# Two-way attention and a two-layer network on one core: the reads' rows reordered and moved ahead of the last token tiles, under a new list of steps

## The chip, the cores and the metric

The kernel runs on one core of a Trainium2 chip. The metric is the device time of one execution in microseconds, lower is better. A core has TensorE (PE in the profile; PEld is its weight load), VectorE (DVE), ScalarE (ACT), GpSimd (POOL), and SyncE (SP), which here only issues DMAs. The DMAs of SP, ACT and POOL run on 16 shared DMA engines. SBUF is the working memory, PSUM holds what PE writes, in eight banks of 2 KB for each of 128 partitions.

## The reference

For each of 8 batches and 8 heads, 512 tokens `x` and 32 states (64 columns each) read one another; the reads of all heads, side by side, pass through two matrices with a PReLU between them.

```python
scores = scale * np.matmul(x, state.transpose(0, 1, 3, 2))
a = softmax(scores); xread = np.matmul(a, state)      # each token reads the states
scores2 = scale * np.matmul(state, x.transpose(0, 1, 3, 2))
a2 = softmax(scores2); sread = np.matmul(a2, x)       # each state reads the tokens
y = np.concatenate([xread, sread], axis=2)            # 8 batches of 512 + 32 rows of 512
h = y @ w_in                                          # 512 -> 2048
g = np.maximum(h, 0.0) + alpha * np.minimum(h, 0.0)
return g @ w_out                                      # 2048 -> 512, 4352 rows
```

## The kernel before

All work is written out by hand as a list, `ORDER`: each token of it (`F.3.1.4`) calls a step with its arguments, and each engine executes its instructions in the order in which the list brings them. Waits between engines follow from the tiles. When an engine waits, all that stands behind it on that engine waits too. Two reads of one PSUM tile by different engines also follow one another in the list's order.

PSUM is given out by number: a step's last figures are banks 0 to 5 (`single`), and one tile of two banks (`two`) serves the scores and some of the `m` steps in turn. A step that takes a bank waits for the last reader of what stood in it.

The steps, for a batch b (0 to 7):
- `lx` loads x (POOL's queue, cast to f16), `wi` and `wo` the four parts of each weight matrix. `xt`/`xo` transpose x on PE and copy it out (batches 0 and 1), `xd` transposes it by a DMA of SP's queue (batches 2 to 7). `stt`, `sto`, `str`, `sro` do the same with the states.
- `sc` computes the scores, states as weights (small matmuls on parts of the array). For the tokens' softmax over the states: `sb` (DVE, blocks transposed), `smax`, `ssh` (subtraction), `sexp` (ACT), `ssum` (sum and reciprocal), `snorm` (POOL or DVE, as the letter says), `wb` (transposed back). Batch 0 does these in two halves of 256 tokens (last figure 0 or 1).
- For the states' softmax over the tokens: `tm` (maximum, DVE), `te` (exponential, ACT), `tsum`, `tn` (POOL), `tt` (a DMA transpose on SP's queue, into the tile `e2T`), `rd` (32 small matmuls, `sr_ps`), `rdo` (copied into `XS`).
- The tokens' reads are never formed: `m` multiplies the states with a quarter f of `w_in` (16 quarter tiles, `mo` copies them out: `mo.b.f.e` in one piece on engine a = ACT or v = DVE, `mo.b.f.e.g` in halves), and the first layer is then attention weights times `m`.
- `F.b.jc.k` (first) makes 128 of the 2048 hidden columns for 512 tokens: two matmuls of 512 columns into bank k. `N` (ACT) takes max(-h, 0), `G` (DVE) adds it, scaled, to h and so frees the bank. `b = 8` stands for the 256 rows of state reads, from `XS`: four matmuls of 256 columns.
- `S.b.q.i` (second) adds hidden columns 2i and 2i+1 to output tile q of 128 tokens: two matmuls of 512 columns. `O` copies the tile out and stores it on SP's queue (256 KB). `R.q.i` and `RO.q` do so for the two tiles of state reads.

Before, the last steps are the token tiles of batch 7, then `R` and `RO`. `RO` copies half of a tile on ACT and half on DVE into one tile `osr` and stores it, 4 batches by 32 states.

Of the kernel before, what the change touches and what calls it, by code (L numbers as in the profile page):

```python
# [17 lines left out]
stc lst stt.0 oma wi.0 sto.a wo.0 xt.0.0.1.0 wi.1 xt.0.0.0.1 xo.0.0.1.v lx.1 xo.0.0.0.v xt.0.1.0.0  # L18
sc.0.0 wo.1 xo.0.1.0.v xt.0.1.1.1 sb.0.0 wi.2 xo.0.1.1.a smax.0.0 wi.3 sc.0.1 str.1.1 sb.0.1
ssh.p.0.0 tm.0 str.0.0 sro.1.a wo.2 smax.0.1 sexp.0.0 m.0.0.1.2 lx.2 sro.0.a ssh.v.0.1 ssum.0.0  # L20
sexp.0.1 m.1.0.0.3 mo.0.0.a.0 mo.0.0.a.1 m.2.0.4.5 snorm.p.0.0 ssum.0.1 te.0.1 m.3.0.1.2 snorm.p.0.1
wb.0.0 te.0.0 lx.3 wb.0.1 mo.1.0.a.0 mo.1.0.a.1 m.4.0 tsum.0 mo.2.0.a.0 mo.2.0.a.1 tn.0.1 F.0.0.0
mo.3.0.a.0 mo.3.0.a.1 m.0.1.4.5 wo.3 F.0.1.3 N.0.0 mo.0.1.a.0 mo.0.1.a.1 tn.0.0 G.0.0 F.0.2.1 N.0.1
F.0.3.0 xt.1.0.0.4 N.0.2 G.0.1 xt.1.1.1.5 tt.0 xt.1.0.1.2 xo.1.0.0.a G.0.2 xo.1.1.1.a F.0.4.3
S.0.0.0.4 N.0.3 xo.1.0.1.v F.0.5.1 N.0.4 G.0.3 xt.1.1.0.2 mo.4.0.a S.0.2.0.5 xo.1.1.0.v S.0.0.1
G.0.4 N.0.5 F.0.6.2 sc.1 G.0.5 N.0.6 m.1.1.3.0 S.0.2.1 mo.1.1.a.0 mo.1.1.a.1 sb.1 F.0.7.1 S.0.2.2
N.0.7 m.0.2.0.3 G.0.6 S.0.0.2 mo.0.2.a.0 mo.0.2.a.1 smax.1 S.0.1.0.2 S.0.1.1 F.0.8.0 G.0.7 ssh.p.1
S.0.1.2 N.0.8 tm.1 S.0.3.0.3 F.0.9.1 S.0.1.3 N.0.9 G.0.8 S.0.3.1 sexp.1 S.0.2.3 G.0.9 F.0.10.0
# [6 lines left out]
N.1.5 S.1.0.1 N.1.6 S.0.1.6 G.1.4 te.2.1 S.0.1.7 G.1.5 F.1.7.5 O.0.1.a m.2.2 G.1.6 N.1.7 F.1.8.1
tsum.2 mo.2.2.a rdo.1.v S.1.1.0.2 tn.2.0 G.1.7 F.1.9.3 N.1.8 smax.2 S.1.1.1 N.1.9 F.1.10.5 xd.4
tn.2.1 S.1.0.2 N.1.10 G.1.8 m.2.1 S.1.0.3 G.1.9 mo.2.1.a F.1.11.1 ssh.p.2 G.1.10 S.1.1.2 N.1.11
F.1.12.3 F.1.13.5 G.1.11 tt.2 N.1.12 S.1.1.3 N.1.13 F.1.14.1 G.1.12 sexp.2 m.2.3 G.1.13 S.1.0.4
F.1.15.3 mo.2.3.a ssum.2 S.1.0.5 S.1.1.4 N.1.14 S.1.1.5 N.1.15 G.1.14 sc.3 snorm.p.2 rd.2.5 xd.5
G.1.15 S.1.0.6 sb.3 S.1.0.7 S.1.1.6 lx.6 O.1.0.a S.1.1.7 wb.2 m.3.1.3.1 S.1.2.0.4 S.1.2.1 rdo.2.v  # L40
smax.3 F.2.0.5 F.2.1.0 N.2.0 S.1.2.2 tm.3 ssh.p.3 N.2.1 S.1.2.3 S.1.2.4 S.1.2.5 G.2.0 te.3.1 S.1.2.6
O.1.1.v S.1.2.7 sexp.3 F.2.2.5 G.2.1 S.1.3.0.2 O.1.2.a ssum.3 S.1.3.1 N.2.2 S.1.3.2 te.3.0 F.2.4.4
S.1.3.3 G.2.2 snorm.p.3 N.2.4 F.2.3.0 tsum.3 mo.3.1.v.0 mo.3.1.v.1 S.1.3.4 N.2.3 F.2.5.5 S.1.3.5
N.2.5 tn.3.1 G.2.4 S.1.3.6 S.1.3.7 G.2.5 F.2.8.4 O.1.3.a G.2.3 m.3.2 tn.3.0 N.2.8 m.3.3.5.1 F.2.6.2
wb.3 mo.3.3.a.0 mo.3.3.a.1 F.2.9.0 S.2.0.0.3 N.2.6 tt.3 G.2.8 S.2.0.1 N.2.9 S.2.1.0.1 G.2.6 F.2.7.4
G.2.9 S.2.1.1 N.2.7 F.2.10.2 mo.3.2.v F.2.11.0 N.2.10 S.2.0.2 N.2.11 S.2.1.2 G.2.7 rd.3.5 G.2.10
F.2.12.4 rdo.3.a lx.7 G.2.11 S.2.0.3 N.2.12 F.2.13.5 S.2.1.3 G.2.12 N.2.13 S.2.0.4 F.2.14.4 G.2.13
S.2.0.5 N.2.14 S.2.1.4 F.2.15.5 G.2.14 S.2.1.5 N.2.15 S.2.0.6 sc.4 G.2.15 S.2.1.6 xd.6 sb.4 S.2.0.7
F.3.0.5 O.2.0.a S.2.1.7 tm.4 N.3.0 F.3.1.4 S.2.2.0.3 N.3.1 F.3.4.0 G.3.0 te.4.1 S.2.2.1 smax.4
S.2.2.2 N.3.4 F.3.2.5 te.4.0 S.2.2.3 G.3.1 ssh.p.4 N.3.2 S.2.2.4 S.2.2.5 G.3.4 F.3.5.4 G.3.2 F.3.3.0  # L50
N.3.5 S.2.2.6 O.2.1.v N.3.3 F.3.6.5 G.3.5 sexp.4 S.2.3.0.1 S.2.3.1 G.3.3 N.3.6 S.2.3.2 tsum.4 ssum.4
# [528 lines left out]
```

## Time and profile before

| | |
|---|---|
| median of 3 runs | 230.43 us (229.63 to 230.91) |
| profiled execution | 230.58 us, its span 228.8 us |
| PE busy | 210.5 us (92%) |
| DVE, ACT, POOL busy | 164.9 (72%), 140.5 (61%), 72.0 (31%) |
| first `F` matmul, last matmul's end | 17.39 us, 220.97 us |

The span runs from the first to the last instruction; 1.8 us of the execution's time lie around it. The idle time of an engine counts only where it delays the end; the chain of waits follows the end back to what released it.

### The profile page before, as it was taken

The page shows a single profiled execution, that of the slowest core. Times are in us where ns is not written, and L with a number is a line of the kernel's source. Part 1 is how long each engine was busy: PE and PEld are TensorE (multiplying, and loading weights), DVE is VectorE, ACT ScalarE, POOL GpSimd, SP SyncE. Part 2 cuts the span into 40 slices and gives each one's busy share as a digit, 9 for nine tenths or more (in the row PEclk, how much of TensorE's full clock was granted, in tenths as well). Part 3 has the DMA queues.
Part 4 walks back from the last instruction along what each step waited for, and adds up shares of the span by engine and source line. Part 5 has one row for each costly group of instructions (what it writes and reads, how often), then busy time and mean ns, then how long its engine had stood idle before and what let it go on. Part 6 is the DMA issues. An engine that isn't in the chain of part 4 may idle for free.

```text
span 228.8 us, 4077 instructions
## 1 busy us (share of the span) xinstructions
PE 210.5 (92%) x1584; PEld 96.5 (42%) x1584; DVE 164.9 (72%) x245; ACT 140.5 (61%) x261; POOL 72.0 (31%) x57
## 2 busy tenths in 40 slices
...
GB/s 69 184 200 199 201 181 192 190 225 185 167 167 106 95 80 149 50 134 56 89 46 138 3 92 0 114 28 47 49 92 47 3 92 0 61 34 92 92 34 57
DMA packets 49051, 23.11 MB, mean 101 GB/s; under 512 B 40456, under 2 KB 44680, under 8 KB 49032
## 3 DMA queue, kind: packets, MB, share of 16 engines
...
q14 instruction: 7, 0.06, 0.1%
...
## 4 chain that ended last, share of the span: by engine, by line
PE 82%; DVE 8%; DMA 3%; ACT 2%; issue 1%; POOL 1%; SPq 0%; POOLq 0%; ACTq 0%
PE o L498 44%; PE h L458 24%; PE m_ps L421 4%; PE h L467 3%; PE o L518 3%; DMA xg<-in_x_dram 2%; PE sr_ps L396 2%; DVE nb L352 2%; DVE gt L486 1%; DMA e2T<-e 1%; PE xT_ps L259 1%; DVE ts L304 1%; PE sc L274 1%; DVE r L328 1%; DVE nb L355 1%
## 5 line engine op out<-in xcount | busy, mean ns | idle before, releaser
L498 PE MATMUL o<-w_out_sb,gt 128*128 128x512 f16 x512 | 130.5, 379 | 0.0
L486 DVE SCALAR_TENSOR_TENSOR gt<-neg,oma_sb,h 128x512 f16<-128x512 f32 x128 | 90.7, 736 | 22.9 <-ACT neg L478 21.6
L478 ACT ACTIVATE neg<-h 128x512 f32<-128x512 f32 (+1 forms) x144 | 80.0, 579 | 40.7 <-PE h L458 34.4
L458 PE MATMUL h<-aT,m 128*128 128x512 f16 x256 | 75.1, 387 | 1.0 <-DVE gt L486 0.7
L498 PEld LDWEIGHTS <-gt 128*128 128x128 f16 x512 | 48.7, 98 | 57.6 <-issue 3.6
L458 PEld LDWEIGHTS <-m 128*128 128x128 f16 x256 | 24.4, 99 | 32.5 <-issue 6.0
L318 POOL TENSOR_TENSOR ts<-ts,mx 128x1024 f32<-128x1024 f32 (+1 forms) x8 | 14.4, 1800 | 53.5 <-DVE mx L312 53.5
L377 POOL TENSOR_SCALAR e<-e,r 128x512 f16<-128x512 f16 x16 | 24.9, 1562 | 5.3 <-DVE r L373 3.0
L508 ACT COPY osb<-o 128x512 f32<-128x512 f32 x25 | 14.5, 591 | 18.7 <-PE o L498 18.4
L332 POOL TENSOR_TENSOR an<-ts,r 128x1024 f16<-128x1024 f32 (+1 forms) x9 | 15.4, 1718 | 22.1 <-DVE r L329 15.5
L421 PE MATMUL m_ps<-w_in_sb,stT 64*32 64x512 f16 x256 | 13.4, 425 | 2.0 <-ACT stT L241 1.3
L447 ACT CAST m<-m_ps 128x512 f16<-128x512 f32 x26 | 13.9, 609 | 1.7 <-PE m_ps L421 1.7
L445 ACT CAST m<-m_ps 128x1024 f16<-128x1024 f32 x13 | 13.2, 1014 | 0.8 <-PE m_ps L421 0.6
L508 DVE COPY osb<-o 128x512 f32<-128x512 f32 x7 | 4.8, 685 | 11.6 <-PE o L498 11.6
L157 POOL DMA_DIRECT2D xg<-in_x_dram x7 | 8.4, 1199 | 12.8 <-PE sr_ps L396 12.8
L363 ACT ACTIVATE e<-sc,nb 128x512 f16<-128x512 f32 x16 | 11.0, 689 | 2.2 <-DVE gt L486 1.2
L304 DVE STREAM_TRANSPOSE ts<-sc 128x1024 f32<-128x1024 f32 x7 | 8.7, 1246 | 3.7 <-PE sc L274 2.9
L340 DVE STREAM_TRANSPOSE aT<-an 128x1024 f16<-128x1024 f16 (+1 forms) x9 | 10.1, 1119 | 1.4 <-POOL an L332 1.2
L328 DVE TENSOR_REDUCE r<-ts 128x32 f32<-128x1024 f32 (+1 forms) x9 | 9.8, 1090 | 1.0 <-ACT ts L324 1.0
L352 DVE TENSOR_REDUCE nb<-sc 128x2 f32<-128x1024 f32 x8 | 9.7, 1208 | 0.5 <-PE sc L274 0.5
L312 DVE TENSOR_REDUCE mx<-ts 128x32 f32<-128x1024 f32 (+1 forms) x9 | 9.8, 1089 | 0.0
L467 PE MATMUL h<-XS,w_in_sb 128*128 128x256 f16 x64 | 8.9, 273 | 0.0
...
## 6 DMA issues: line engine op xcount, KB each, us to landing
out_dram<-osb SPq DMA_DIRECT2D x32, 256.0 KB, 2.0
...
xg<-in_x_dram POOLq DMA_DIRECT2D x2, 256.0 KB, 5.0
out_dram<-osr SPq DMA_DIRECT2D x2, 256.0 KB
...
e2T<-e SPq DMA_TRANSPOSE x8, 3.1
```

Of the source, the lines that this page charges most:

```text
L318: engine(e).tensor_tensor(ts, ts, over_blocks(cols(live["mx", b], j, S // N)), ALU.subtract)
L332: engine(e).tensor_tensor(blocks(cols(live["an", b], j, S)), blocks(cols(live["ts", b], j, S)), over_blocks(cols(live["r1", b], j, S // N) ...
L352: nc.vector.tensor_reduce(nb, live["sc", b].rearrange("p r j g s -> p g (r j) s"), AX.XY, ALU.max)
L377: nc.gpsimd.tensor_scalar_mul(e2, e2, live["r2", b][:, g : g + 1])
L421: nc.tensor.matmul(t[N * k : N * (k + 1), :], st_head(b, h)[64 * r : 64 * r + 64, :], w_in_sb[64 * r : 64 * r + 64, c, 512 * f : 512 * (f ...
L447: copier(e)(m_tile(b)[:, f, g, :], t[g])
L458: nc.tensor.matmul(h.rearrange("p (r j s) -> p r j s", r=2, j=2), ms[b][:, f, g, 128 * j : 128 * (j + 1)], weights(b, g), start=(g == 0), ...
L467: nc.tensor.matmul(h, w_in_sb[:, c, 128 * jc : 128 * (jc + 1)], XS[:, c, :, :].rearrange("p b n -> p (b n)"), start=(c == 0), stop=(c == n ...
L478: nc.scalar.activation(neg, h, RELU, bias=0.0, scale=-1.0)
L486: nc.vector.scalar_tensor_tensor(gt, negs.pop((b, jc)), oma_sb[:, jc : jc + 1], h, ALU.mult, ALU.add)
L498: nc.tensor.matmul(outs[b, q], gts[b, jc][:, 128 * q : 128 * (q + 1)], w_out_sb[:, jc, :], start=(jc == 0), stop=(jc == n_jc - 1),)
L508: copier(e)(osb, outs.pop((b, q)))
```

## The change

- All places in `ORDER` are new: the steps are nearly the same, but their order, PSUM banks and engines (a, v, p) are others.
- Three `F` steps of batch 0 become six `f` steps (`first_part`), each for one half of 256 tokens, so that the first half needs only `wb.0.0`.
- `XS` keeps the state reads as (half of the batches, state, batch in the half), so output tile q of `R` has its 128 rows in the order state, batch. `RO` copies a whole tile on one engine, and its store goes by 32 states, 4 batches.
- `R` and `RO` stand between the `S` steps of batch 7. The last step is now `O.7.3.s`: two halves of the columns, one copied by ACT and stored from ACT's queue, one copied by DVE and stored from SP's.

```diff
-    XS = consts.tile([128, n_c, B, N], F16)
+    XS = consts.tile([128, n_c, 2, N, B // 2], F16)
...
-        copier(e)(XS[:, :, b, :], live.pop(("sr", b)))
+        copier(e)(XS[:, :, b // 4, :, b % 4], live.pop(("sr", b)))
...
-                    XS[:, c, :, :].rearrange("p b n -> p (b n)"),
+                    XS[:, c].rearrange("p q n b -> p (q n b)"),
...
+    def first_part(b, jc, j, k=None):
+        if ("part", b, jc) not in live:
+            live["part", b, jc] = hs[b, jc] = single(k, f"h_{b}_{jc}", [128, S], F32)
+        f, i = divmod(jc, 4)
+        for g in range(2):
+            nc.tensor.matmul(
+                hs[b, jc].rearrange("p (r j s) -> p r j s", r=2, j=2)[:, :, j, :],
+                ms[b][:, f, g, 128 * i : 128 * (i + 1)],
+                weights(b, g)[:, :, j, :],
...
     def second_out(b, q, e):
...
+        if e == "s":
+            for i, (c, n) in enumerate((("a", nc.scalar), ("v", nc.sync))):
+                osb = moe.tile([128, w], F32, name=f"osb_{b}_{q}_{i}", tag="osr", bufs=2)
+                copier(c)(osb, t[:, w * i : w * (i + 1)])
+                n.dma_start(rows[:, w * i : w * (i + 1)], osb)
+            return
...
-    def second_reads_out(q):
-        w = d_model // 2
-        osb = moe.tile([128, d_model], F32, name=f"osr_{q}", tag="osr", bufs=2)
-        nc.scalar.copy(osb[:, :w], outs[B, q][:, :w])
-        nc.vector.tensor_copy(osb[:, w:], outs[B, q][:, w:])
-        nc.sync.dma_start(out.rearrange("(b s) d -> b s d", s=S2)[4 * q : 4 * (q + 1), S:], osb)
+    def second_reads_out(q, e):
+        osb = moe.tile([128, d_model], F32, name=f"osr_{q}", tag="osb", bufs=4)
+        copier(e)(osb, outs.pop((B, q)))
+        rows = out.rearrange("(b s) d -> b s d", s=S2)[4 * q : 4 * (q + 1), S:]
+        nc.sync.dma_start(rows.rearrange("b n d -> n b d"), osb)
```

Of the list, the end reads now:

```diff
-S.7.3.7 R.0.0.0 O.7.3.v R.0.1 R.0.2 R.0.3 R.0.4 R.0.5 R.0.6 R.0.7 R.1.0.2 RO.0 R.1.1 R.1.2 R.1.3
-R.1.4 R.1.5 R.1.6 R.1.7 RO.1
+S.7.2.3 R.1.6 S.7.2.4 R.1.7 S.7.2.5 RO.1.v S.7.2.6 S.7.2.7 S.7.3.0.2 O.7.2.v S.7.3.1 S.7.3.2 S.7.3.3
+S.7.3.4 S.7.3.5 S.7.3.6 S.7.3.7 O.7.3.s
```

**The end, DVE's queue.** `osr` are the read tiles, `osb` the token tiles, `o_7_3` the PSUM tile of the last token step; the brackets name whom a row waits for. Before:

```order
L486 SCALAR_TENSOR_TENSOR gt_7_14_2809<-neg_7_14_2799,oma_sb_84,h_7_14_2790 128x512 [waits Activation_49]
L486 SCALAR_TENSOR_TENSOR gt_7_15_2817<-neg_7_15_2811,oma_sb_84,h_7_15_2803 128x512 [waits Activation_49]
L508 COPY osb_7_3_2887<-o_7_3_2852 128x512 [waits DMAHW3_49,DMAHW7_49,DMAHW1_49,PE_49]
L530 COPY osr_0_2907<-o_8_0_2884 128x256 [waits Activation_49]
L530 COPY osr_1_2925<-o_8_1_2904 128x256 [waits Activation_49]
```

After:

```order
L501 SCALAR_TENSOR_TENSOR gt_7_11_2835<-neg_7_11_2828,oma_sb_84,h_7_11_2823 128x512 [waits Activation_49]
L550 COPY osr_0_2853<-o_8_0_2805 128x512 [waits DMAHW3_49,DMAHW6_49,DMAHW0_49,PE_49]
L550 COPY osr_1_2913<-o_8_1_2874 128x512 [waits DMAHW5_49,DMAHW3_49,DMAHW7_49,DMAHW2_49,PE_49]
L532 COPY osb_7_2_2923<-o_7_2_2896 128x512 [waits DMAHW4_49,DVE_49,PE_49]
L528 COPY osb_7_3_1_2943<-o_7_3_2920 128x256 [waits Activation_49]
```

The last half copy on DVE waits for ACT in both; the tile is now a token tile, and the read tiles stand ahead of it.

**The start, DVE's queue, batch 0.** `r1` are the sums of the two halves, `an` the normalized weights, `aT` the weights turned back (`wb`). Before:

```order
L328 TENSOR_REDUCE r1_0_146<-ts_0_144 128x16 [waits Activation_49]
L329 RECIPROCAL r1_0_146<-r1_0_146 128x16 [waits DVE_49]
L328 TENSOR_REDUCE r1_0_146<-ts_0_144 128x16 [waits Activation_49]
L329 RECIPROCAL r1_0_146<-r1_0_146 128x16 [waits DVE_49]
L340 STREAM_TRANSPOSE aT_0_148<-an_0_147 128x512 [waits Pool_49] x2
L373 RECIPROCAL r2_0_253<-r2_0_253 128x2 [waits Activation_49]
```

After:

```order
L329 TENSOR_REDUCE r1_0_146<-ts_0_144 128x16 [waits Activation_49]
L330 RECIPROCAL r1_0_146<-r1_0_146 128x16 [waits DVE_49]
L341 STREAM_TRANSPOSE aT_0_148<-an_0_147 128x512 [waits Pool_49]
L333 TENSOR_TENSOR an_0_147<-ts_0_144,r1_0_146 128x512 [waits DVE_49]
L374 RECIPROCAL r2_0_261<-r2_0_261 128x2 [waits Activation_49]
L341 STREAM_TRANSPOSE aT_0_148<-an_0_147 128x512 [waits DVE_49]
L446 CAST m_4_293<-m_ps4_0_271 128x1024 [waits PE_49]
```

The second half's normalization moved from POOL to DVE, between the two transposes, and a cast of `m` follows.

**The start, ACT's queue.** `ts` are the exponentials of the two halves (`sexp`), `m_0` the casts `mo.0.0`. Before:

```order
L324 ACTIVATE ts_0_144<-ts_0_144 128x512
L447 CAST m_0_236<-m_ps0_0_0_209 128x512
L447 CAST m_0_236<-m_ps0_0_1_210 128x512
L363 ACTIVATE e2_0_252,r2_0_253<-sc_0_120,nb_0_187 128x512 x2
L447 CAST m_1_271<-m_ps1_0_0_226 128x512
```

After:

```order
L448 CAST m_0_223<-m_ps0_0_0_210 128x512
L448 CAST m_0_223<-m_ps0_0_1_211 128x512
L325 ACTIVATE ts_0_144<-ts_0_144 128x512
L364 ACTIVATE e2_0_260,r2_0_261<-sc_0_120,nb_0_203 128x512 x2
L448 CAST m_1_268<-m_ps1_0_0_228 128x512
```

The second half's exponential now stands behind the two casts.

**Batch 2's transposes, SP's queue.** Before:

```order
L511 DMA out_0_dram<-osb_0_1_779 128x512
L251 DMA_TRANSPOSE xT_4_820<-xg_4_732 128x16x128
L381 DMA_TRANSPOSE e2T_2_861<-e2_2_742 128x8x128
L251 DMA_TRANSPOSE xT_5_957<-xg_5_745 128x16x128
L511 DMA out_0_dram<-osb_1_0_975 128x512
```

After:

```order
L533 DMA out_0_dram<-osb_0_3_775 128x512
L382 DMA_TRANSPOSE e2T_2_869<-e2_2_704 128x8x128
L252 DMA_TRANSPOSE xT_4_884<-xg_4_778 128x16x128
L252 DMA_TRANSPOSE xT_5_981<-xg_5_798 128x16x128
L533 DMA out_0_dram<-osb_1_0_998 128x512
```

`e2T_2`, which the state reads of batch 2 need, changed places with `xT_4`.

## Rows read from the trace of the kernel before

**Rows 1.** The page's busy time of each engine (us, share of the span, instructions)

```profile
PE 210.5 (92%) x1584; PEld 96.5 (42%) x1584; DVE 164.9 (72%) x245; ACT 140.5 (61%) x261; POOL 72.0 (31%) x57
```

**Rows 2.** The chain in order of time: start us, us, what

```profile
17.39 1.03 PE h L458 x2
...
19.08 2.67 PE h L458 x6
...
22.70 0.43 PE h L458 x2
...
151.37 0.54 PE o L498 x2
...
214.04 6.92 PE o L518 x32
...
220.99 0.38 ACT osr L529
...
221.39 0.42 DVE osr L530
```

**Rows 3.** Windows: stretch, its us, busy us of each engine, PEclk, DMA

```profile
19.08:21.75 2.67, 2.67 (x8) 0.99 (x9) 1.12 (x2) 2.67 (x6) 2.63 (x3) 1.00 1.27 206
...
62.20:130.00 67.80, 67.76 (x493) 29.97 (x494) 60.06 (x85) 44.66 (x83) 23.13 (x14) 1.00 0.48 97
142.00:201.00 59.00, 59.00 (x429) 29.24 (x428) 45.94 (x74) 39.76 (x76) 10.65 (x7) 1.00 0.17 55
```

**Rows 4.** Timeline of PE: start us, us, instruction, [idle before and releaser]

```profile
50.58 0.59 PE L458 MATMUL h<-aT,m 128*128 128x512 f16 x2 [0.65 <-DVE gt L486]
...
61.50 0.68 PE L396 MATMUL sr_ps<-e2T,xg 128*64 128x32 f16 x32 [0.88 <-DMA e2T<-e]
```

**Rows 5.** Windows of the tail; the last two figures: DMA share, GB/s

```profile
214.80:216.40 1.60, 1.60 (x9) 0.73 (x8) 0.00 (x0) 0.00 (x0) 0.00 (x0) 1.00 0.79 298
222.20:227.20 5.00, 0.00 (x0) 0.00 (x0) 0.00 (x0) 0.00 (x0) 0.00 (x0) 0.64 0.25 84
227.20:228.80 1.60, 0.00 (x0) 0.00 (x0) 0.00 (x0) 0.00 (x0) 0.00 (x0) 0.50 0.00 0
```

**Rows 6.** Timeline of DVE: the copy of the last token tile

```profile
214.08 0.69 DVE L508 COPY osb<-o 128x512 f32<-128x512 f32 x1 [11.57 <-PE o L498]
```

**Rows 7.** DMA issues on the page: KB each, median us to landing

```profile
out_dram<-osb SPq DMA_DIRECT2D x32, 256.0 KB, 2.0
```

**Rows 8.** DVE's groups by form: count, busy us, mean ns, idle before

```profile
L445 DVE CAST m<-m_ps 128x1024 f16<-128x1024 f32 x2 | 2.4, 1218 | 0.0
...
L508 DVE COPY osb<-o 128x512 f32<-128x512 f32 x7 | 4.8, 685 | 11.6 <-PE o L498 11.6
...
L318 DVE TENSOR_TENSOR ts<-ts,mx 128x512 f32<-128x512 f32 x1 | 0.7, 693 | 0.0
```

**Rows 9.** Timeline of the start, all engines

```profile
13.54 0.63 ACT L324 ACTIVATE ts<-ts 128x512 f32<-128x512 f32 x1
...
14.07 1.05 ACT L447 CAST m<-m_ps 128x512 f16<-128x512 f32 x2
...
14.54 2.05 POOL L332 TENSOR_TENSOR an<-ts,r 128x512 f16<-128x512 f32 x2 [1.44 <-DVE r L329]
...
16.52 0.63 PE L421 MATMUL m_ps<-w_in_sb,stT 64*32 64x512 f16 x8 [0.73 <-ACT e L363]
...
16.62 0.71 DVE L340 STREAM_TRANSPOSE aT<-an 128x512 f16<-128x512 f16 x1 [0.29 <-POOL an L332]
```

**Rows 10.** Timeline of SP's queue

```profile
54.68 3.46 SPq L251 DMA_TRANSPOSE xT<-xg  x1
58.23 1.26 SPq L381 DMA_TRANSPOSE e2T<-e  x1
```

**Rows 11.** Timeline of POOL: the scaling of batch 2

```profile
52.02 3.10 POOL L377 TENSOR_SCALAR e<-e,r 128x512 f16<-128x512 f16 x2 [3.03 <-DVE r L373]
```

**Rows 12.** Timeline of DVE at the wait of 50.6 us

```profile
48.65 1.25 DVE L304 STREAM_TRANSPOSE ts<-sc 128x1024 f32<-128x1024 f32 x1 [0.82 <-ACT e L363]
```

More of the change, by code (lines that the diff above doesn't have):

```diff
@@ L17 @@
 ORDER = """
[L18 to L28, printed above, removed]
@@ L35 @@
[L35 to L45, printed above, removed]
@@ L46 @@
[L46 to L51, printed above, removed]
@@ new lines @@
+N.1.15 ssum.2 S.1.1.4 S.1.1.5 S.1.0.6 S.1.1.6 G.1.14 snorm.p.2 sc.3 m.3.1.4.2 G.1.15 rd.2.0 xd.5
+mo.3.1.a.0 mo.3.1.a.1 sb.3 S.1.0.7 S.1.1.7 lx.6 rdo.2.a O.1.0.a m.3.2.0.2 tm.3 m.3.3.4.1 S.1.2.0.3
+mo.3.2.a.0 mo.3.2.a.1 S.1.2.1 wb.2 S.1.2.2 te.3.1 S.1.2.3 te.3.0 S.1.2.4 smax.3 F.2.0.0 mo.3.3.a.0
+mo.3.3.a.1 F.2.4.2 S.1.2.5 tsum.3 N.2.0 ssh.p.3 O.1.1.v F.2.1.1 N.2.4 G.2.0 S.1.2.6 N.2.1 S.1.3.0.5
+G.2.4 F.2.5.0 tn.3.0 G.2.1 sexp.3 S.1.3.1 F.2.2.2 F.2.6.1 N.2.5 ssum.3 S.1.3.2 tn.3.1 N.2.2 S.1.3.3
```

137 lines of the change are left out of this document (83 added, 54 removed).

## Prediction

> **What bounds the kernel now.** I read the busy table first, then the chain, then the windows, then the waits. TensorE (PE) is busy 92% of the span, VectorE (DVE) 72% [rows 1]. Since a busy PE need not be PE at its peak, I checked its pace: from 21.75 us on a pair of 512-column matmuls takes 0.43 us again and again [rows 2], that is 216 ns for 512 columns, the 2.4 GHz level, and the windows show PE without idle time except two stretches [rows 3]. These are 0.65 us at 50.6 us, where a first-layer matmul waits for DVE, and 0.88 us at 61.5 us, where the state reads wait for a DMA transpose [rows 4]. So between 21.75 and 220.97 us a new list can win about 1.6 us and little more, unless it shrinks PE's own work. It can lose any amount.
>
> What is left lies at the two ends. At the front the first `F` starts at 17.39 us, and its matmuls take 445 ns each until 21.75 us (2.67 us for six) [rows 2]: that is the 1.2 GHz level, although the window prints a granted clock of 1.00 there [rows 3]. At the back PE ends at 220.97 us [rows 2], and the span ends at 228.8: 7.8 us in which no matmul runs.
>
> **The tail, step by step.** Before: ScalarE (ACT) copies half of the last reads tile, 0.38 us, then DVE the other half, 0.42, one after the other, to 221.81 [rows 2]. Then SP issues a store that moves 84 GB/s at 0.25 of the 16 DMA engines; nothing moves after 227.2, and 1.6 us of closing follow [rows 5]. The token store, equal in bytes, goes quicker: two of them, the second issued when DVE's copy ended at 214.77 [rows 6], move 298 GB/s at 0.79 of the engines up to 216.4 [rows 5], some 1.6 us after that issue; such a store lands in 2.0 [rows 7]. The slow store has 4 as its outermost count (4x32x512), the quick one 128; the share of a quarter fits 4 engines of 16.
>
> After: the last thing is the token tile `O.7.3.s`, in two column halves of 128 rows each, on two queues, and both read stores went out before it. The copies still run in turn, for the DVE half waits on `Activation` in the new order; I book nothing for parallel copies. ACT's half is issued about 0.45 us before DVE's and is off the path. So: PE end + 0.84 (copies) + 0.03 + 1.6 (issue to last byte, a whole tile's time taken for a half, as the nearest row) + 1.6 (closing) = 4.1 us instead of 7.8: **-3.8 us**. The better bound: a half moves in half the time, about 0.4 less: -4.2. The worse: the read stores (32x4x512, a shape that no row shows) stay at a quarter of the engines and delay what is queued behind them on SP, or the halves do; 128 KB at 84 GB/s is 1.5 us instead of 0.4 at 298: -2.8. I take -3.8, since 32 rows of the outer count are nearer to 128 than to 4.
>
> That a quarter share goes with an outer count of 4 is what the row shows. The Trainium skill, page "DMA: Bandwidth & Descriptors", section "Why a DMA increments its semaphore by 16 and not by 1", says that a transfer is dealt to the largest number of engines, up to 16, that divides the slowest dimension of both sides. For 4x32 this is 4, and the trace agrees (0.25); for 32x4 it would be 16, and no run here shows that yet. By the rule the worse bound falls away; without it the bound stays, as rival A.
>
> The read tiles' own copies (now whole, on DVE, 0.685 us each [rows 8]) and stores lie under the 70 and 22 matmuls that follow them on PE (15.1 and 4.8 us). The 32 `R` matmuls only move; their 6.92 us [rows 2] are paid either way. `XS` in another order means strided writes of 128 columns on ACT or DVE; even at the price of a copy four times as long (0.685) they are covered while the new list has 1.3 us of PE work (three 0.43 us units) between `rd.7` and `F.8.0`, the tightest place.
>
> **The start, step by step.** The new list puts both `mo.0.0` casts (1.05 us) ahead of `sexp.0.1` on ACT, which before ran at 13.54 [rows 9]. So `sexp.0.1` ends near 15.1 and not 14.2, and the second sum, of 0.9 us, ends at 16.0 on DVE. `wb.0.0` is now queued behind that sum and ends at 16.7. Then the second half is normalized on DVE (a form that no row shows; bounds 0.69, DVE's subtraction of that width [rows 8], and 1.03, half of POOL's pair [rows 9]; I take 0.69), and `wb.0.1` ends at 18.3 instead of 17.33 (16.62 + 0.71): 1 us later. This is what the half-width `f` steps cover. `f.0.0.0` needs only the first half, and PE comes free when `m.4.0` ends (16.52 + 0.63) [rows 9]: start at 17.15, before 17.39. From there, at the low clock (223 ns for 256 columns): two first halves to 18.05, a hole to 18.3, four more half steps to 20.1, `m.0.1` and `m.1.1` to 21.4, `F.0.3` at 21.4. Before, at 21.75, `F.0.3` was done, but not `m.1.1`. Following `N`, `G` and the x copies at their durations to 26.1 us, I find eight `F` and three `S` done, against seven `F`, three `S` and `sc.1`: 0.1 us ahead. But `sc.1` then waits for the cast of `m.1.1`, queued on ACT behind `N.0.5`, until about 26.4. Net **+0.2 us**, between -0.3 and +1.0 (the lateness of `wb.0.1` in full). The weights' DMAs change places on POOL: `wo.2` ahead of `wi.3`, `wo.3` ahead of `lx.3`; the parts needed first come first, and `lx.3` serves batch 3 only, so nothing is booked.
>
> **The body.** In the SP queue the transpose of `e2T_2` now stands ahead of `xT_4`. Before, its input was ready at 55.1, when POOL's scaling ended, but it was issued at 58.23, when `xT_4`, issued at 54.68 and 3.46 us in the queue, was through [rows 10, 11]. Three microseconds earlier more than cover the 0.88 that PE waited: **-0.9**. The other wait: DVE idles 0.82 us for ACT ahead of `sb.2`, and the `G` behind it releases the bank [rows 12]. Now three `G` stand between `tm.2` and `sb.2`, and `F` goes round three PSUM banks instead of two: 0 to -0.65, I take **-0.3**. There the late one is next: `F.1.7` waits for the third of these `G`, about 0.3; with `sc.1` **+0.6** of new waits, bounds 0 and 2. And wherever PE turns from small-tile matmuls (m, sc, rd, xt) to full ones, the next pair takes 0.54 instead of 0.43 [rows 2]; the list has 25 such groups instead of 29: **-0.4**.
>
> Sum: -3.8 + 0.2 - 0.9 - 0.3 - 0.4 + 0.6 = -4.6 us. The profiled execution took 230.58 us (span 228.8, 1.8 around it): 226.0. The median of the three runs is 0.15 lower, which I leave inside the rounding: **226.0 us**, about -1.9%.
>
> **Rivals.**
> A, the tail is not what it seems: the reads or the halves are still dealt to few engines, gain 2.8 instead of 3.8: 227.0. For it: no row shows the shape. Against: the token stores of 128 rows.
> B, the clock comes late: the hole at 18.05 and the shifted start delay the rise to 2.4 GHz. Before, PE was dense for 4.4 us (17.39 to 21.75) before its pace doubled; if as long a stretch more were run at half pace, 2.2 us are lost: 228.2. Against: PE has fewer than 0.3 us of holes there.
> C, slower than before: DVE becomes the bound in batches 1 to 6. It is 60.06 us busy in 67.8 [rows 3], and gets more: three more two-bank casts (1.218 each), three more output copies (0.685), two whole read copies for two halves (0.685 against 0.42) and the one normalization (0.69): +6.9 us [rows 8], before some smaller copies that leave it. A late `G` holds a bank, and `F` waits as at 50.6. It decides from about 5.8 us of new waits on. At two such waits of 0.65 in each of six batches (7.8) the time is 230.58 - 4.6 + 7.8 = 233.8. Against: in the new list an `F` comes back to a bank no sooner than 1.3 us of PE work after its last use, and the 6.9 us face 13.1 us of idle DVE between 142 and 201 us alone [rows 3].
> D, the same but mild: 3.5 to 5.5 us of such waits: within 0.5%, about 230.
>
> **How the numbers follow.** Forecast 0.76, A 0.07, B 0.07, C 0.05, D 0.05. The range: from 224.4 (tail -4.2, start -0.3, no new waits) to 228.2 (B; A with late first weights lies below it); C and D stay outside. About 0.5% (1.15 us) is what a measurement can tell from no change. Faster: forecast, A and most of B, 0.87; same: D and the rest of B, 0.07; slower: C and a little of D, 0.06.
>
> **What would show it.** PE's last matmul to the span's end near 4.1 us (A: over 5); the read stores at some 0.8 of the DMA engines; the DVE half still behind ACT's; the first `h` matmuls near 17.2 and a hole of some 0.3 us at 18; pairs of 0.43 from about 22 us (B: from later); no `sr_ps` wait for e2T at 61; under 1.5 us of PE waits behind 22 us, so that PE ends at 219.8 to 220.7 (C: 226 or later, with `h` waiting for `gt`). Wrong would be the whole sum if PE's end moved by over 2 us either way.

## The result

| | before | after |
|---|---|---|
| median of the runs, us | 230.28 (229.63 to 230.91, 4 runs) | 224.56 (224.13 to 225.14, 4 runs) |
| profiled execution, us | 230.58 | 224.41 |
| its span, us | 228.8 | 222.6 |
| PE's last matmul ends, us | 220.97 | 218.64 |
| from there to the span's end, us | 7.8 | 4.0 |

The ratio is 0.975 with a 95% interval of 0.972 to 0.979: faster by 5.7 us, where 4.4 were forecast (226.0). Two executions in what follows, one of the kernel before at 370 us and one of the kernel with `O.2.0` earlier at 366 us, were slow ones at a granted clock near 0.58, and the ranges and ratios leave them out. In the profiled executions the 6.2 us of span are 3.87 us behind the last matmul and 2.33 us ahead of it. The forecast had 3.8 for the first and 0.8 for the second: the tail came as worked out, the list gave more than I booked.

The chain of waits of the kernel after, where it answers to [rows 2] (start us, us, what):

```profile
17.39 2.79 PE h L481 x12
...
213.87 4.76 PE o L513 x22
```

The start looks as before, but for 12 half-width `h` matmuls in place of the first full ones. At the end stand the last 22 matmuls of the token tiles, not the 32 `R` matmuls. What follows them is in the timeline of ACT, DVE and the DMA queues of ACT (ACTq) and SP (SPq) after 213 us (start us, us, instruction, idle before it and its releaser):

```profile
218.66 0.37 ACT L528 COPY osb<-o 128x256 f32<-128x256 f32 x1 [8.44 <-PE o L513]
219.06 0.36 ACTq L529 DMA_DIRECT2D out_dram<-osb  x1
219.06 0.42 DVE L528 COPY osb<-o 128x256 f32<-128x256 f32 x1 [3.17 <-ACT osb L528]
219.51 0.33 SPq L529 DMA_DIRECT2D out_dram<-osb  x1
```

DVE's copy still starts when ACT's ends, though the two write different tiles. The windows of the tail (the last two figures are the DMA share and GB/s):

```profile
219.80:220.60 0.80, 0.00 (x0) 0.00 (x0) 0.00 (x0) 0.00 (x0) 0.00 (x0) 1.00 0.76 259
220.60:221.40 0.80, 0.00 (x0) 0.00 (x0) 0.00 (x0) 0.00 (x0) 0.00 (x0) 1.00 0.21 69
```

The DMA issues of the page (KB each, median us to landing):

```profile
out_dram<-osr SPq DMA_DIRECT2D x2, 256.0 KB, 2.5
...
out_dram<-osb ACTq DMA_DIRECT2D x1, 128.0 KB, 1.8
out_dram<-osb SPq DMA_DIRECT2D x1, 128.0 KB, 1.9
```

Where [rows 5] had 84 GB/s at 0.25 of the engines for 5 us, the two last half stores now move 259 GB/s at 0.76. In slices of 0.1 us the last byte moves at 220.9, 1.7 us ahead of the span's end; before it was 1.6. The read stores land in 2.5 us.

One thing in [rows 5] is easily misread: 84 GB/s for 5 us are 420 KB, more than the 256 KB of one store. The window also holds the end of the first read store, issued at 218.39. The last store was issued at 221.84 and needed 5.3 us to its last byte at 227.2; in slices of 0.4 us neither of the two moves over 102 GB/s, at 0.26 of the engines.

The body, in two of the windows of [rows 3]:

```profile
62.20:130.00 67.80, 67.24 (x486) 30.12 (x485) 60.49 (x87) 42.61 (x82) 23.13 (x15) 1.00 0.52 98
142.00:201.00 59.00, 59.00 (x419) 29.69 (x417) 45.86 (x70) 38.27 (x77) 8.14 (x5) 1.00 0.16 50
```

PE's timeline at the two places behind 30 us where it waits, and at the reads of batch 2 (the waits stand in brackets with their releaser):

```profile
32.63 0.59 PE L459 MATMUL h<-aT,m 128*128 128x512 f16 x2 [0.38 <-DVE gt L501]
...
61.08 0.68 PE L397 MATMUL sr_ps<-e2T,xg 128*64 128x32 f16 x32
...
87.78 1.02 PE L513 MATMUL o<-w_out_sb,gt 128*128 128x512 f16 x4 [0.56 <-ACT osb L532]
```

The two waits of [rows 4] are gone. Two new ones stand elsewhere: 0.38 us for a `G`, and 0.56 us for a bank that the copy of `O.2.0` holds. That copy is queued on ACT behind the second half of the exponential, `te.4.0`. DVE, 60.06 us busy in the first window before, has 60.49.

To see where the list gained, I counted PE's work ahead of a few steps in both lists (0.432 us for a pair of 512-column matmuls, 0.28 for a group of eight `m` matmuls, 0.56 for `rd`, 0.22 for `sc` and for `xt`, and 0.17 for each turn from small tiles to full ones; these are estimates from the traces' rows) and took it from the time at which the step runs. What is left is the time lost up to there. In the profile after, the second part of the first `x` arrived 0.29 us later (`sc.0` at 8.45 instead of 8.16), which I take out as chance: over all profiles `sc.0` starts at 7.98 to 8.16 with the list before and at 7.96 to 8.61 with the new one.

| time lost up to | before | after | change |
|---|---|---|---|
| `sc.1` | 16.62 | 16.05 | -0.57 |
| `sc.2` | 16.68 | 16.64 | -0.04 |
| `sc.3` | 17.54 | 16.67 | -0.87 |
| `sc.4` | 18.52 | 16.65 | -1.87 |
| `sc.7` | 19.26 | 17.35 | -1.91 |
| PE's end | 19.27 | 17.30 | -1.97 |

With 0.65 us less counted work (25 turns instead of 29) this makes -2.62 us, and +0.29 for the later `x` gives the 2.33 seen. A part of it is the chance of this pair of profiles: counted from `sc.0`, PE ends at 212.0 to 212.8 us in the four profiles with the list before (mean 212.4), and at 210.0 to 210.6 in the seven that keep the new list's half steps and its place of the reads (mean 210.3). That makes 2.1 us.

### The profile page after: what moved, and what is told of

It reads as the page before. It is cut to its first block, busy times and chain, and to the rows that moved or that the text cites. A ratio compares the mean times of both kernels' runs of the same rounds, so it can differ in the third digit from the quotient of the medians.

```text
span 222.6 us, 4094 instructions
## 1 busy us (share of the span) xinstructions
PE 208.7 (94%) x1590; PEld 97.4 (44%) x1590; DVE 168.1 (76%) x248; ACT 136.3 (61%) x263; POOL 70.9 (32%) x56
## 4 chain that ended last, share of the span: by engine, by line
PE 84%; ACT 5%; DVE 5%; DMA 2%; issue 1%; POOL 0%; ACTq 0%; POOLq 0%
PE o L513 46%; PE h L459 22%; PE m_ps L422 3%; PE h L468 3%; PE o L540 3%; DMA xg<-in_x_dram 2%; PE sr_ps L397 2%; DVE gt L501 2%; ACT neg L493 1%; PE h L481 1%; PE sc L275 1%; DVE ts L305 1%; DVE nb L353 1%; ACT stT L242 1%; ACT e L364 1%
## 5 line engine op out<-in xcount | busy, mean ns | idle before, releaser
L501 DVE SCALAR_TENSOR_TENSOR gt<-neg,oma_sb,h 128x512 f16<-128x512 f32 x128 | 89.7, 735 | 17.5 <-ACT neg L493 16.3
L493 ACT ACTIVATE neg<-h 128x512 f32<-128x512 f32 (+1 forms) x144 | 78.7, 585 | 34.2 <-PE h L459 30.3
L459 PE MATMUL h<-aT,m 128*128 128x512 f16 x250 | 70.8, 381 | 0.4 <-DVE gt L501 0.4
L448 ACT CAST m<-m_ps 128x512 f16<-128x512 f32 x38 | 20.1, 605 | 11.5 <-PE m_ps L422 11.5
L532 ACT COPY osb<-o 128x512 f32<-128x512 f32 x21 | 12.5, 596 | 11.6 <-PE o L513 11.6
L333 POOL TENSOR_TENSOR an<-ts,r 128x1024 f16<-128x1024 f32 (+1 forms) x8 | 14.4, 1801 | 8.5 <-DVE r L330 4.8
L422 PE MATMUL m_ps<-w_in_sb,stT 64*32 64x512 f16 x256 | 12.8, 431 | 2.1 <-ACT e L364 1.2
L550 DVE COPY osr<-o 128x512 f32<-128x512 f32 x2 | 1.4, 691 | 12.6 <-PE o L540 12.6
L325 ACT ACTIVATE ts<-ts 128x1024 f32<-128x1024 f32 (+1 forms) x9 | 8.7, 966 | 1.2 <-POOL ts L319 1.2
```

What stands on the lines that cost most here:

```text
L333: engine(e).tensor_tensor(blocks(cols(live["an", b], j, S)), blocks(cols(live["ts", b], j, S)), over_blocks(cols(live["r1", b], j, S // N) ...
L422: nc.tensor.matmul(t[N * k : N * (k + 1), :], st_head(b, h)[64 * r : 64 * r + 64, :], w_in_sb[64 * r : 64 * r + 64, c, 512 * f : 512 * (f ...
L448: copier(e)(m_tile(b)[:, f, g, :], t[g])
L459: nc.tensor.matmul(h.rearrange("p (r j s) -> p r j s", r=2, j=2), ms[b][:, f, g, 128 * j : 128 * (j + 1)], weights(b, g), start=(g == 0), ...
L493: nc.scalar.activation(neg, h, RELU, bias=0.0, scale=-1.0)
L501: nc.vector.scalar_tensor_tensor(gt, negs.pop((b, jc)), oma_sb[:, jc : jc + 1], h, ALU.mult, ALU.add)
```

## Experiments

Theory: two separate gains. The tail's comes from what is stored last and how its rows are dealt to the DMA engines. The list's comes from waits and turns of PE. Rivals: that the tail is not paid by the store, that the list gives nothing, or that the `f` steps, the split last copy or ACT's new order at the start are what counts. Each ratio is to the kernel before on the same chip. The kernel before had medians of 229.86 to 230.28 us beside them.

### Which part of the tail: rows or order

**Rows alone, in the kernel before** (its list, with `R` last):

```diff
-    XS = consts.tile([128, n_c, B, N], F16)
+    XS = consts.tile([128, n_c, 2, N, B // 2], F16)
...
-        copier(e)(XS[:, :, b, :], live.pop(("sr", b)))
+        copier(e)(XS[:, :, b // 4, :, b % 4], live.pop(("sr", b)))
...
-        nc.sync.dma_start(out.rearrange(...)[4 * q : 4 * (q + 1), S:], osb)
+        rows = out.rearrange(...)[4 * q : 4 * (q + 1), S:]
+        nc.sync.dma_start(rows.rearrange("b n d -> n b d"), osb)
```

> The kernel before with the rows' order alone: XS and the two read stores as in the changed kernel (32 states by 4 batches), the old list, the reads still last and still copied in two halves. My theory (the last store is slow because it runs on a quarter of the DMA engines): PE ends as before near 221.0, the read stores move some 300 GB/s, and the span ends about 4.1 us after PE instead of 7.8: 226.6 us, -3.7. Rival (the store is slow because it is last, or since its bytes come late, whatever its rows): 230.3, no change.

227.07 us (226.69 to 228.25), ratio 0.986 (0.981 to 0.991). Window of its tail:

```profile
222.20:223.30 1.10, 0.00 (x0) 0.00 (x0) 0.00 (x0) 0.00 (x0) 0.00 (x0) 1.00 0.62 238
```

The same 256 KB, to the same rows of the output, move in a window of 1.1 us once the outermost count is 32 and not 4. From its issue (221.28) to its last byte (223.3) the last store takes 2.0 us instead of 5.3, and these 3.3 us are what the tail loses: from the last matmul (220.40) to the span's end are 4.5 us instead of 7.8. The 0.62 and 238 GB/s are means over a window with both of its edges; in slices of 0.1 us between 222.5 and 223.1 the store moves 328 to 430 GB/s at 0.87 to 1.10 of the engines. By the Trainium skill, page "DMA: Bandwidth & Descriptors", section "Why a DMA increments its semaphore by 16 and not by 1", 32x4 would be dealt to 16 engines. The trace agrees: these slices have no less than the token stores, which reach 1.08 in slices of 0.2 us before.

**The old rows, in four DMAs, in the kernel before:**

```diff
-        nc.sync.dma_start(out.rearrange(...)[4 * q : 4 * (q + 1), S:], osb)
+        rows = out.rearrange(...)[4 * q : 4 * (q + 1), S:]
+        for i in range(4):
+            nc.sync.dma_start(rows[i], osb[N * i : N * (i + 1), :])
```

> The kernel before with each read store issued as four DMAs of 32 rows by 512 (one for each batch) instead of one of 4 by 32; the rows' order and all else as before. If the outermost count decides how many DMA engines a store gets: the bytes move at over 200 GB/s on most engines, the span ends about 4.1 us after PE plus three more issues on SP (0.33 each): 227.0 to 227.6 us. If the old order of the rows itself (32 neighbouring rows at a time) makes the store slow: 229.9 to 230.5.

227.12 us (226.59 to 228.3), ratio 0.985 (0.979 to 0.992). Last matmul to end: 220.03 to 224.8, 4.8 us. The queue and the windows:

```profile
220.91 1.72 SPq L533 DMA_DIRECT2D out_dram<-osr  x4
```

```profile
222.00:222.40 0.40, 0.00 (x0) 0.00 (x0) 0.00 (x0) 0.00 (x0) 0.00 (x0) 1.00 0.63 154
222.40:224.00 1.60, 0.00 (x0) 0.00 (x0) 0.00 (x0) 0.00 (x0) 0.00 (x0) 0.66 0.34 88
```

The same bytes in the same order gain 3 us in the tail, only by being cut so that no DMA has an outermost count of 4. So neither the bytes nor their addresses made the store slow. The issue of four DMAs costs 1.72 us and eats a part; 64 KB in each 0.43 us of issue are 152 GB/s, so by this estimate the issue sets the pace of the first window.

**Order alone, in the kernel before:** both `R` tiles ahead of `S.7.2` and `S.7.3`, stores with the old rows.

```diff
-... S.7.1.7 S.7.2.0.0 O.7.1.a ... S.7.3.7 R.0.0.0 O.7.3.v R.0.1 ... R.1.7 RO.1
+... S.7.1.7 O.7.1.a R.0.0.3 R.0.1 ... R.1.7 RO.1 S.7.2.0.0 ... S.7.3.7 O.7.3.v
```

> The kernel before with the place alone: the reads' second layer moved ahead of the last two token tiles (S.7.2, S.7.3), rows and stores as before (4 batches by 32 states), the last token tile stored whole. If the two parts of the tail's change are two ways to one gain: the slow store has 6.9 us of matmuls to run under, the last token tile's copy (0.7) and store end about 4.0 us after PE: 226.5 us. Rival (what is queued behind a slow store on SP's queue is held up): over 5.5 us after PE, 228 us or more.

226.28 us (226.06 to 226.52), ratio 0.982 (0.978 to 0.986). End of its chain:

```profile
206.57 6.91 PE o L518 x32
213.47 6.92 PE o L498 x32
220.42 0.69 DVE osb L508
```

Span 224.4: 4.0 us behind the last matmul, with the slow stores still in the program but hidden under 6.92 us of matmuls.

**The kernel after with the old rows:**

```diff
-    XS = consts.tile([128, n_c, 2, N, B // 2], F16)
+    XS = consts.tile([128, n_c, B, N], F16)
...
-        nc.sync.dma_start(rows.rearrange("b n d -> n b d"), osb)
+        nc.sync.dma_start(rows, osb)
```

> The changed kernel with the rows' order undone: XS and the read stores as before (4 by 32), all else as changed. One-gain theory: the slow stores run under the last token tiles, the end shifts by 0 to 0.4 us: 224.6 to 225.0. Rival (the rows' order carries the tail's gain, or the slow store delays the last one): 1 us and more, 225.6 to 228.

224.57 us (224.37 to 224.75), ratio 0.974 (0.969 to 0.979): the kernel after was 224.56. Rows and order are two ways to the same 3.3 to 3.9 us of the profiled tail (2.8 and 3.6 us in the medians); given the order, the rows move the time by nothing that can be measured. In the profile the two half stores land later with the old rows (2.5 and 2.4 us against 1.8 and 1.9 above), and the tail is 4.5 us instead of 4.0; that half microsecond does not show in the medians.

### What the list is worth without the tail

**The kernel after with `R` last,** old rows and old read copies. In the first version I only took the `R` steps out from between the others:

```diff
-F.7.15.1 R.0.0.3 G.7.10 N.7.15 R.0.1 S.6.3.7 G.7.15 R.0.2 O.6.3.a F.7.11.1 R.0.3 ... O.7.3.s
+F.7.15.1 G.7.10 N.7.15 S.6.3.7 G.7.15 O.6.3.a F.7.11.1 ... S.7.3.7 R.0.0.0 O.7.3.v R.0.1 ... R.1.7 RO.1
```

> The changed kernel's list with the end of before: reads last, two half copies into one tile, rows 4 by 32. It shows what the new list is worth without the tail. If tail and list add up: PE ends near 218.6, the span 7.8 later: 228.4 us (2.1 below before). If the list's gain hangs on the new end: 230.

230.26 us (229.64 to 231.03), ratio 1.000 (0.998 to 1.003). It reads as if the list gave nothing. PE's timeline, with the idle time ahead of each, shows why:

```profile
199.07 0.59 PE L459 MATMUL h<-aT,m 128*128 128x512 f16 x2 [1.04 <-DVE gt L501]
...
207.24 7.07 PE L513 MATMUL o<-w_out_sb,gt 128*128 128x512 f16 x32 [0.67 <-ACT osb L532]
```

My edit made these: without the `R` steps between, `F.7.11` comes to its bank before DVE has freed it, and an `S` tile to one that ACT still copies. So the run doesn't price the list; what it shows is that the reads between the last token tiles serve as filler while banks come free. The second version gives `F.7.11` and the last tiles other banks, and works the `S.7` tiles in pairs as the kernel before does:

```diff
-F.7.15.1 R.0.0.3 G.7.10 N.7.15 R.0.1 S.6.3.7 G.7.15 R.0.2 O.6.3.a F.7.11.1 R.0.3 N.7.11 S.7.0.0.2 ...
+F.7.15.1 G.7.10 N.7.15 S.6.3.7 G.7.15 O.6.3.a F.7.11.4 N.7.11 S.7.0.0.5 G.7.11 S.7.0.1 S.7.1.0.3 ...
```

> The changed kernel's list with the end of before once more, without the waits that my first version had brought in: its last first-layer step took a bank whose reader came just ahead of it, and the last tiles stood one after another. Now F.7.11 and the tiles of S.7 take banks long free (4, 5, 3, 2), and the S.7 tiles alternate in pairs as in the old list; reads last, stores 4 by 32. If list and tail add up: PE ends near 219.0, 227.0 to 228.5 us. If the reads between the S steps are what the new list's end lives on: 229.5 or more, with PE waiting after its last F.

228.13 us (227.61 to 228.7), ratio 0.988 (0.981 to 0.996). The end of the chain is the old one:

```profile
212.09 6.92 PE o L540 x32
```

PE ends at 219.01 and the span at 226.9: 7.9 us of tail, as before. So the list alone gives 2.1 us of the 5.7 by the medians of 230.28 and 228.13, as by the ends of PE above; the interval of the ratio leaves 1.0 to 4.3.

**Full `F` steps for the half-width ones:**

```diff
-f.0.0.0.2 wb.0.1 tn.0.0 f.0.1.0.3 ... f.0.0.1 f.0.1.1 f.0.2.0.4 f.0.2.1 N.0.0
+wb.0.1 tn.0.0 ... F.0.0.2 F.0.1.3 F.0.2.4 N.0.0
```

> The changed kernel with full F steps in place of the six half-width f steps of batch 0 (they stand where the second halves stood, after wb.0.1). If the half steps cover the late second half of the weights, as I worked out: the first h matmul moves from 17.3 to about 18.3 us, the time is 0.6 to 1.0 us longer, 225.2 to 225.6. Rival (ACT and DVE, not PE, set the pace of the start, so PE's early work only moves a wait): 224.5, with the wait later.

225.37 us (224.9 to 226.77), ratio 0.978 (0.971 to 0.985). PE's timeline:

```profile
17.91 2.74 PE L459 MATMUL h<-aT,m 128*128 128x512 f16 x6 [0.93 <-DVE aT L341]
```

That is the late second transpose that the prediction spoke of. `sc.1` runs 18.88 us behind `sc.0` here and 17.66 in the kernel after, so the half steps are worth 1.2 us there, and 0.8 in the medians, which the wide run at 226.77 blurs.

**ACT's order at the start:** `sexp.0.1` ahead of the two `mo.0.0` casts, as in the kernel before.

```diff
-mo.0.0.a.0 mo.0.0.a.1 ssum.0.0 m.1.0.2.3 m.2.0.4.5 sexp.0.1
+sexp.0.1 mo.0.0.a.0 mo.0.0.a.1 ssum.0.0 m.1.0.2.3 m.2.0.4.5
```

> The changed kernel with the second exponential of batch 0 ahead of the two casts of m again, as in the old list; ACT's queue alone changes. If that order costs what I worked out (wb.0.1 1 us later) and f covers it: wb.0.1 about 0.6 us earlier, the time the same within 0.3, 224.3 to 224.9. If the late second half is on the path: 223.6 to 224.0.

224.19 us (223.88 to 224.85), ratio 0.972 (0.966 to 0.978), between the two times expected. PE's end is 210.1 us behind `sc.0`, as in the kernel after (210.2): with the half steps, the later `sexp.0.1` costs nothing that can be measured.

### The last tile, and a version that may beat both

**The last tile unsplit,** `O.7.3.a` for `O.7.3.s`:

> The changed kernel, but its last token tile goes out whole: one copy of 128x512 on ACT and one store on SP, instead of two column halves copied by ACT and by DVE and stored on two queues. In the changed kernel the two half copies run one after the other (0.38 and 0.42 us), since the DVE half waits for ACT, and two stores of 128 KB follow; one whole copy on ACT took 0.59 us in the kernel before and one store of 256 KB landed in about 2 us. Theory: the split is worth nothing, because the copies do not run side by side: 224.6 us within 0.3. Rival: the halves on two queues land earlier than one whole store, and the split is worth 0.4 us or more: 225.0 or above.

224.26 us (223.9 to 224.76), ratio 0.976 (0.974 to 0.978). ACT's copy in its timeline:

```profile
219.09 0.59 ACT L532 COPY osb<-o 128x512 f32<-128x512 f32 x1 [8.48 <-PE o L513]
```

The span ends at 223.0, 4.0 us behind the last matmul: the split is worth nothing, since its copies run in turn (0.38 + 0.42 us against 0.59).

**The halves as two accumulators in two banks,** so that ACT's copy runs beside the second half's matmuls:

```diff
-S.7.3.0.2 O.7.2.v S.7.3.1 ... S.7.3.7 O.7.3.s
+O.7.2.v T.7.3.0.0 T.7.3.1.1
...
+    def last_half(b, q, i, k):          # T: 16 matmuls of 256 columns, copy, store
...
+        t = single(k, f"o_{b}_{q}_{i}", [128, w], F32)
+        for jc in range(n_jc):
+            nc.tensor.matmul(t, gts[b, jc][...], w_out_sb[:, jc, w * i : w * (i + 1)], ...)
...
+        copier("av"[i])(osb, t)
+        (nc.scalar, nc.sync)[i].dma_start(rows[:, w * i : w * (i + 1)], osb)
```

> The changed kernel, but the two column halves of its last token tile are two accumulators in two PSUM banks, worked one after the other with 8 matmuls of 256 columns each, so that the copy of the first half by ACT runs beside the matmuls of the second. Theory: the copies of the changed kernel run in turn because both read one tile; with two tiles only DVE's 0.42 us is left behind the last matmul, 0.4 us less: 224.15 us (last matmul to the span's end 3.6 instead of 3.96). Rival: 16 matmuls of 256 columns cost more than 8 of 512, and eat the gain: 224.5 or more.

(A half has 16 matmuls, not the 8 written there: 32 in all instead of 16.) 224.04 us (223.53 to 224.37), ratio 0.975 (0.973 to 0.977). The end of its chain:

```profile
215.18 3.51 PE o L539 x32
218.69 0.02 issue
218.71 0.42 DVE osb L549
```

DVE's copy follows the last matmul at once, and the span ends 3.5 us behind it instead of 4.0. The 32 narrow matmuls take 3.51 us, where 16 wide ones take 3.45 in the chain of the kernel after. The 0.45 us are plain in the profile; of the medians, 0.2 to 0.5 less than the unsplit tile and the kernel after, they are no proof.

**The copy of `O.2.0` earlier on ACT:**

```diff
-te.4.0 S.2.1.6 smax.4 O.2.0.a
+O.2.0.a te.4.0 S.2.1.6 smax.4
```

> The changed kernel with one entry of its list moved: the copy of the token tile O.2.0 stands ahead of the second mask multiplication te.4.0 on ACT instead of two places behind it. In the trace of the changed kernel PE waits 0.6 us at 87.8 us for that copy, which is queued on ACT behind an operation that itself waits for GpSimd. Theory: the copy no longer waits, the 0.6 us of PE idle time go, and nothing else comes late: 224.0 us. Rival: the hole is taken up again by the next bank that is late, so that the end doesn't move: 224.5.

223.82 us (223.80 to 224.09), ratio 0.974 (0.973 to 0.976). PE's timeline:

```profile
88.66 0.59 PE L513 MATMUL o<-w_out_sb,gt 128*128 128x512 f16 x2 [0.68 <-ACT osb L532]
```

The rival held. The wait at 87.78 is gone and the next bank is late instead, 1.3 us further on (counted from `sc.0`) and 0.1 longer: its copy, `O.2.1`, stands behind `te.4.0` and two `N`. (The expectation calls `te.4.0` a mask multiplication that waits for GpSimd. It is the exponential, and in the trace of the kernel after ACT waits there 0.90 us for DVE's `sb`.) PE's end is 0.2 us nearer to `sc.0` than in the kernel after; the rest of the 0.7 us in the medians I can't put down to the edit, since in its profile `sc.0` starts 0.4 us earlier.

**Both edits:**

> The changed kernel with both edits, the two accumulators of the last token tile and the earlier copy of O.2.0. If each gives what its theory says, 0.4 and 0.6 us, they lie in different stretches and add up: 223.5 us. If one of them is given back, 223.9 to 224.2.

223.68 us (223.52 to 223.96), ratio 0.973 (0.971 to 0.975), the lowest median of all. Its advantage over the kernel after (0.9 us) is not beyond what the two intervals leave open; what the profiles carry of it is the 0.4 us of the second accumulator.

## The prediction, point by point

The direction, the place of the larger gain and the range held; 1.3 us of gain were not foreseen. By the prediction's last sign the sum is nevertheless wrong: PE's end moved by 2.33 us in the two profiles, over the 2 us that it named as the limit, and 218.64 lies below its 219.8 to 220.7. The tail's half of the sum came true by its steps; the list's half was mis-sized, 0.8 us booked against 2.1 in the runs, and the time came near because the tail is the larger part.

**The tail: right, by its own steps.** 4.07 us were worked out from the last matmul to the end, 3.96 measured: 0.84 for the copies, 1.4 from the issue to the last byte (1.6 booked) and 1.7 of closing (1.6 booked). The copies ran in turn, as the wait for ACT in the order had said. The 84 GB/s that it gave to one store are the pace of a window with parts of two, which changes nothing in the sum. The reason held as well: the runs with other rows, with four DMAs and with another order each take 3 us and more off the tail. What the prediction did not say is that order and rows are each enough: it named the rows for a bound only, and the row order could have been left alone. The read stores reach the 0.8 of the engines that it named as a sign (0.61 and 1.04 in the two slices of 0.4 us that hold most of the first one with the rows alone). Rival A is out.

**The start: booked at +0.2 with +0.3 for `sc.1`; measured -0.57 up to `sc.1`, and -0.04 at `sc.2`.** The first `f` started at 17.32 (17.15 worked out, and `x` came 0.29 late). Timeline of DVE:

```profile
16.30 0.65 DVE L341 STREAM_TRANSPOSE aT<-an 128x512 f16<-128x512 f16 x1
16.87 0.65 DVE L333 TENSOR_TENSOR an<-ts,r 128x512 f16<-128x512 f32 x1
17.44 0.15 DVE L374 RECIPROCAL r<-r 128x2 f32<-128x2 f32 x1
17.55 0.71 DVE L341 STREAM_TRANSPOSE aT<-an 128x512 f16<-128x512 f16 x1
```

The second half's normalization takes 0.65 (0.69 booked), and the second transpose ends at 18.26, where 18.3 was worked out for an `x` that came 0.29 sooner. The hole of 0.3 us on PE did not come: each row of this timeline starts up to 0.1 us before the end of the one ahead, which a sum of durations leaves out, and at 233 ns a matmul instead of 223 the first two half steps are just done by 18.26. `sc.1` did not wait for the cast that I feared; 0.38 us for a `G` at 32.63, ahead of `sc.2`, took its place; all ten profiles of the new list have it, at 0.33 to 0.38.

**The wait for `G` at 50.6: mis-sized.** Booked -0.3, and +0.3 for `F.1.7` close behind; measured -0.83 between `sc.2` and `sc.3`, and no wait left. The four profiles with the list before have it at 0.65 or 0.66, none of the ten with the new list has it. I gave the third bank half of what it brought, and then charged a wait that did not come.

**The transpose of `e2T_2`: right in size by luck, wrong in its reason.** It was issued at 55.16 instead of 58.23, three microseconds earlier, as worked out. It did not land three microseconds earlier: the step that failed is the one from an earlier issue to an earlier landing. SP's queue, and the DMA issues between 54 and 62 us of the kernel after (median us to landing):

```profile
55.16 1.24 SPq L382 DMA_TRANSPOSE e2T<-e  x1
56.85 6.74 SPq L252 DMA_TRANSPOSE xT<-xg  x2
```

```profile
q0 software_dynamic: 3171, 0.80, 101.1%
q1 hardware_dynamic: 3126, 0.79, 56.6%
...
e2T<-e SPq DMA_TRANSPOSE x1, 5.7
```

The same view of the kernel before:

```profile
q1 hardware_dynamic: 3364, 1.07, 80.9%
q0 software_dynamic: 1068, 0.27, 33.9%
...
e2T<-e SPq DMA_TRANSPOSE x1, 3.1
```

The term that I left out is on POOL's queue. The loads of `x` for batches 4 and 5 wait for the reads of batches 0 and 1, and these moved behind in the list. Timeline of POOL, before and after:

```profile
46.60 2.39 POOL L157 DMA_DIRECT2D xg<-in_x_dram  x2 [7.19 <-PE sr_ps L396]
```

```profile
49.53 2.38 POOL L158 DMA_DIRECT2D xg<-in_x_dram  x2 [9.07 <-PE sr_ps L397]
```

Issued 2.9 us later, these loads are in flight beside the transpose (the POOL queue's packets take three times the share), which lands in 5.7 us instead of 3.1: at 60.9 instead of 61.3. I followed the steps past SP's queue and not past POOL's. Over the transpose's own time from issue to landing, POOL's queue moves nothing in the four profiles with the list before, and 0.56 to 0.60 MB in the ten with the new one. That the loads slow the transpose is still read from the traces side by side; no run moves the loads alone, so the cause stays open. The two `xT` transposes issued behind it are a rival, since they are in flight beside it too; against them, the transpose landed soonest (5.3 us, with `O.2.0` earlier) where they were issued soonest behind it (1.3 us) and latest (6.6, `R` last with other banks) where they were issued 2.4 us behind it.

What the other traces do show is that the 0.9 was the chance of one profile. Counted from `sc.0`, the transpose landed at 52.2 to 53.2 us with the list before and, without the run with full `F` steps, at 51.8 to 53.3 with the new one. With the list before PE waited for it 0, 0.25, 0.40 and 0.88 us; with the new list not at all in five profiles and 0.28 to 0.75 in five. In three of these five the profile names a `G` instead (0.35, 0.44, 0.35), but in all five the `sr_ps` matmuls start some 0.15 us after the landing. On the average the new place is worth 0.2 us. PE's end in the three edits of the kernel before, 212.0 to 212.4 us behind `sc.0` instead of 212.8, says the same.

**Turns of PE: mis-sized.** Booked -0.4 at the 0.11 us that the next pair takes longer; by the count of the lists above a turn costs some 0.17, which makes -0.65. The 0.06 between the two is that count's, and no row shows it by itself.

**Rival B (late clock): out.** PE's timeline after:

```profile
17.32 2.86 PE L481 MATMUL h<-aT,m 128*128 128x256 f16 x12
20.11 1.05 PE L422 MATMUL m_ps<-w_in_sb,stT 64*32 64x512 f16 x16
21.10 1.04 PE L459 MATMUL h<-aT,m 128*128 128x512 f16 x2
21.93 0.53 PE L260 MATMUL xT_ps<-ident,xg 128*128 128x128 f16 x4
22.29 0.59 PE L459 MATMUL h<-aT,m 128*128 128x512 f16 x2
22.73 0.61 PE L260 MATMUL xT_ps<-ident,xg 128*128 128x128 f16 x8
```

The 12 halves take 233 ns each in the chain, the pair at 21.10 still has 1.04 us, the one at 22.29 leaves PE 0.44 later: the 2.4 GHz level comes at about 22, as before, with PE busy without a hole from 17.32. The windows print a granted clock of 1.00 on both sides of it.

**Rivals C and D (DVE the bound): out.** I had priced DVE's additional work at 6.9 us; over the whole span it is 3.2:

```profile
PE 208.7 (94%) x1590; PEld 97.4 (44%) x1590; DVE 168.1 (76%) x248; ACT 136.3 (61%) x263; POOL 70.9 (32%) x56
```

Counting what is added and not what goes to ACT doubles the price. Of waits of PE two are left, 0.38 us for a `G` and 0.56 for a copy on ACT. Whether 6.9 us more on DVE would have brought others, no run shows.

**The strided copies into `XS`** went from 0.27 to 0.43 us on DVE and from 0.28 to 0.49 on ACT, inside the bound of 0.685, and no wait of PE names them.

Put together: the booked list gain of 0.8 became 2.62 at equal arrival of `x`: 0.54 more at the start and its waits, 0.83 at the wait for `G`, 0.25 of turns, 0.1 at the transpose and 0.1 behind `sc.4`. Behind `sc.4` the new wait at 87.78 is set off by small losses of before that its trace shows as no idle time, since the ends of PE's matmuls are modelled; what these were stays open. In the runs the list is worth 2.1 us, so some 0.5 of the 2.62 is the chance of this pair, the transpose's share above all.
